# A soft-threshold on ScalarE with its halves moved by transfers, two small routing operations dropped, and more pauses

## The chip, the cores and the metric

The kernel runs on one core of a Trainium2 chip. The metric is the device time of one execution in microseconds; each figure is the median of several. A core has TensorE (PE), VectorE (DVE), ScalarE (ACT), GpSimd (POOL), SyncE (SP) and 16 DMA engines, each engine with its own queue of instructions.

## The reference

Three parts follow each other. The second and third are called moe and moe2 in the code.

```python
X = np.fft.rfft(x, axis=1)                      # x: 8 batches x 3072 x 256
Yr = Xr @ w_r - Xi @ w_i + b_r                  # Yi alike
Yr = np.sign(Yr) * np.maximum(np.abs(Yr) - 0.01, 0.0)
y = np.fft.irfft(Yr + 1j * Yi, n=3072, axis=1)  # 24576 tokens x 256
h = np.maximum(y @ w_in, 0.0)                   # 256 x 2048
z = h * h @ w_out                               # 2048 x 256
logits = z @ w_gate                             # 8 experts
# the first `capacity` (768) tokens of each expert, in order of tokens, keep a slot
out[i] = gate_w[i] * (np.maximum(z[i] @ w1[e], 0.0) @ w2[e])   # kept tokens; else 0
```

## The kernel before

The FFT of a batch runs as two matrix stages with a turn through DRAM between them, the inverse likewise: s1 (x to u), s2 (u to the complex spectrum, `a` and `sm`), mix_a and mix_b (the products with w_r and w_i and the soft threshold, result y), sa (y to z) and sb (z to yT, the tokens of the batch). A batch has 24 indices j for s2 and sa, and 12 pairs k of them for the mix. The first half of the mix (mix_a) adds the bias on VectorE, the second (mix_b) adds its products, so that t = [128, 2, 256] holds the real and the imaginary part. The soft threshold is t - clip(t): VectorE clips t into c (L373), and four GpSimd subtractions of 64x256 (L378) write the halves of t - c, moved to other partitions, into two tiles y. The program's name for the ring of y is `xc`, for t and c it is `ue`, since they share memory with other rings.

The tokens go through in 48 blocks of 512, six a batch. For each block, 16 times (f), l1 makes 128 rows of h: six matmuls, then ScalarE's Relu (L556) and Square (L557). Blocks 0 to 10 are full: l2 follows for each f. From block 11 on a block is late: only the logits are made, by l2_gate, which takes four f at a time (at f=6, 10 and 14, and the last four at f=2 of the next block), twelve bf16 matmuls (L596). They read h*h in three parts: the top half of its bits, what VectorE's first subtraction leaves (L560), and what a second subtraction leaves of that (L561); in the latter, E_POOL names the f that GpSimd does, the others are VectorE's. Both subtractions are emitted one f later (DELAY). route works out the slots of the block before in some 25 small operations, five per f, and four scatters (L663, indirect DMAs issued by GpSimd) follow at f=9.

The FFT of the next batch runs between the l1 of the blocks. A list of steps is handed out by fft_share at an even pace over the blocks of a batch, so that the last step falls at f=6 of the batch's last block; in late blocks f=2, 5 and 10 have no step, and theirs follow at the block's end. From batch 2 on the steps begin at the third block of a batch. So the first two blocks of batches 2 to 5 have no FFT steps; here they are called bare. The list is written by fft_ahead (s1, then load_first, which loads the first spectrum tiles `uj`, then GAP empty steps) and fft_mid (for each pair: two s2, two sa of the pair two before, mix_a, mix_b; some empty steps at the end). Every engine works through its queue in order, so the order of the steps is the order of the work. When all experts are full, the rest is skipped: here the kernel leaves the blocks at f=9 of block 31.

In late blocks l1 has three PSUM tiles, and the FFT steps, route and the transposes share four in turn.

Of the kernel before, what the change touches and what calls it, by code (L numbers as in the profile page):

```python
# [8 lines left out]
F32 = mybir.dt.float32  # L9
F32R = mybir.dt.float32r  # L10
BF16 = mybir.dt.bfloat16
I32 = mybir.dt.int32
U32 = mybir.dt.uint32
AF = mybir.ActivationFunctionType
ALU = mybir.AluOpType
AX = mybir.AxisListType
# [3 lines left out]
P = 128  # L20
N1, N2 = 96, 32
LAM = 0.01
BLK = 512
# [4 lines left out]
def fft_mix__moe__moe2_kernel(  # L28
# [20 lines left out]
    nc = tc.nc  # L49
# [26 lines left out]
    UEX = 1  # L76
    SKIP = ((2, 5, 10), (14, 15))
    E_POOL = (0, 1, 2, 4, 5, 6, 8, 9, 10, 12, 13, 14)
    FROM = 2
    FFT_END = 6  # L80
    GAP = 6
    NPRE = 4
    MV = 4
    OUT_FIRST = (1, 2, 3)
# [38 lines left out]
    one = big.tile([P, P], BF16, name="one")  # L123
    desc = big.tile([P, E], F32, name="desc")
    ebase = big.tile([P, E], F32, name="ebase")
    tid = big.tile([P, TPB], I32, name="tid")
    cnt = big.tile([P, E], F32, name="cnt")
    lcnt = big.tile([P, 1], F32, name="lcnt")
    nlate = big.tile([P, 1], I32, name="nlate")
    oh5 = big.tile([P, TPB + 1, E], BF16, name="oh5")  # L130
    kp5 = big.tile([P, TPB + 1], BF16, name="kp5")
    flag = big.tile([P, 1], I32, name="flag")

    class Fft:
        pass
# [216 lines left out]
    def mix_b(st, k, which):  # L352
        a, sm = st.ab.pop(k)
        p = psum_tile(which)
        t = st.t
        if k == 0:
            products(
                p[0:64, D:2 * D],
                0,
                lambda l, h: a[:, l, 2 * h:2 * h + 2, :].rearrange("p r c -> p (r c)")[:, ::4],  # L360
            )
        products(p[:, 0:D], 0, lambda l, h: sm[:, l, h, :])
        nc.vector.tensor_tensor(
            t, p[:, 0:D].unsqueeze(1).to_broadcast([P, 2, D]), t, op=ALU.add
        )
        if k == 0:
            for r in range(2):
                q = slice(32 * r, 32 * r + 1)
                nc.vector.tensor_tensor(
                    t[0:1, r, :], p[q, D:2 * D], bias[q, 0, :], op=ALU.add  # L370
                )
        c = r_c()
        nc.vector.tensor_scalar(c, t, -LAM, LAM, op0=ALU.max, op1=ALU.min)  # L373
        for n in range(2):
            y = r_y()
            src = slice(64 * n, 64 * n + 64)
            for r in range(2):
                y_eng[n == r].tensor_tensor(  # L378
                    y[64 * r:64 * r + 64, :], t[src, r, :], c[src, r, :], op=ALU.subtract
                )  # L380
            st.y[2 * k + n] = y

# [151 lines left out]

    rest_q = []

    def l1(ys, f, late=False, n_tok=BLK, hook=None):
        yh, yl = ys
        p = psum_tile(1)[:, 0:n_tok]
        order = [(0, yh, 0), (0, yh, 1), (1, yh, 0), (1, yh, 1)]  # L540
        low = [(0, yl, 0), (0, yl, 1)]
        order = low + order if f == KF - 1 else order + low
        for n, (l, y, k) in enumerate(order):
            nc.tensor.matmul(  # L544
                p,
                wi_s[:, l, k, f * P:(f + 1) * P],
                y[:, k, 0:n_tok],
                start=(n == 0),
                stop=(n == 5),
            )  # L550
        if hook:
            hook()
        if late:
            s, d = W.ls(), W.ld()
            e = top(d, 0)
            nc.scalar.activation(s, p, AF.Relu)  # L556
            nc.scalar.activation(s, s, AF.Square)  # L557

            def rests():
                nc.vector.tensor_tensor(d, s, top(s), op=ALU.subtract)  # L560
                (gp if f in E_POOL else ve).tensor_tensor(e, d, top(d), op=ALU.subtract)  # L561

            rest_q.append(rests)
            if len(rest_q) > DELAY:
                rest_q.pop(0)()
            return top(s), top(d), e
        s = W.wk3.tile([P, n_tok], F32, tag="s", name="s")
        nc.scalar.activation(s, p, AF.Relu)  # L568
        sh = W.wk3.tile([P, n_tok], F32R, tag="d", name="sh")
        sl = W.wk3.tile([P, n_tok], F32R, tag="d", name="sl")  # L570
        nc.scalar.activation(sh, s, AF.Square)  # L571
        nc.vector.tensor_tensor(s, s, s, op=ALU.mult)  # L572
        nc.vector.tensor_tensor(sl, s, sh.bitcast(F32), op=ALU.subtract)  # L573
        return sh, sl
# [15 lines left out]
    def top(t, w=1):  # L590
        return t.bitcast(BF16).rearrange("p (n w) -> p n w", w=2)[:, :, w]
# [44 lines left out]
    def small(shape, dt, tag):  # L636
        return W.wk1.tile([P] + shape, dt, tag=tag, name=tag)
# [43 lines left out]
    def route(i, zt, lg, lt):  # L681
# [4 lines left out]
        def op(f, *a, **k):  # L686
            ops.append(lambda: f(*a, **k))  # L687
# [41 lines left out]
        op(v.tensor_reduce, sm, w, axis=AX.X, op=ALU.add)  # L729
        op(v.tensor_scalar, sm, sm, 1e-9, None, op0=ALU.add)  # L730
        op(v.reciprocal, zt[:, :, D], sm)
        op(v.tensor_scalar, zi[:, :, D + 1], tid, i * BLK, None, op0=ALU.add)
        ops += [None, places]
        op(v.scalar_tensor_tensor, ok, pos[:, 0:TPB, :], float(cap), oh, op0=ALU.is_lt, op1=ALU.mult)
        if lt is not None:
            kf = small([TPB], F32, "kf")
            op(v.tensor_reduce, kf, ok, axis=AX.X, op=ALU.add)
            op(v.tensor_copy, kp5[:, 0:TPB], kf)
        op(v.tensor_copy, cnt, pos[:, TPB, :])
        op(v.tensor_reduce, mn, cnt, axis=AX.X, op=ALU.min)  # L740
        op(v.tensor_scalar, flag, mn, float(cap), None, op0=ALU.is_lt)
# [79 lines left out]
    def setup_c():  # L821
        nc.gpsimd.memset(zero, 0.0)
        nc.vector.memset(oh5, 0.0)
        nc.vector.memset(kp5, 0.0)
        nc.vector.memset(lcnt, 0.0)
        nc.vector.memset(nlate, 0)
        nc.vector.memset(cnt, 0.0)
        nc.vector.memset(flag, 1)
        nc.vector.memset(one, 1.0)
        nc.vector.memset(wgate, 0.0)  # L830
        nc.gpsimd.memset(tri, 1.0)
        nc.gpsimd.affine_select(
            out=tri, in_=tri, pattern=[[1, P]], compare_op=ALU.is_gt, fill=0.0,
            base=0, channel_multiplier=-1,
        )
        for e in range(E):
            nc.gpsimd.memset(desc[:, e:e + 1], float(E - e))
            nc.gpsimd.memset(ebase[:, e:e + 1], float(e * cap - BIG))
        nc.gpsimd.iota(tid, pattern=[[P, TPB]], base=0, channel_multiplier=1)

    def late_rows(c, rows):
        nc.sync.dma_start(
# [70 lines left out]
    def fft_mid(st):  # L913
        NP = NJ // 2
        nothing = [lambda: None] * 2

        def a2(j):
            if j % 2 == 0 and 2 <= j < NJ - 2:
                load_j(st, j + 2)
            s2(st, j, 0)  # L920

        def sa2(j):
            sa(st, j, 0)
            if j % 2 and j + 5 < NJ:
                load_m(st, j + 5)

        def both(f, k):
            return [lambda j=2 * k + n: f(j) for n in range(2)]

        seq = both(a2, 0) + nothing  # L930
        for k in range(NP):
            if k + 1 < NP:
                seq += both(a2, k + 1)
            seq += both(sa2, k - 2) if k >= 2 else nothing
            seq += [lambda k=k: mix_a(st, k, 0), lambda k=k: mix_b(st, k, 0)]
        return seq + nothing + both(sa2, NP - 2) + both(sa2, NP - 1)

    def sb_steps(st):
        def step(c):
# [21 lines left out]
    with tc.manual_schedule():  # L961
# [165 lines left out]
        for i in range(NBLK):  # L1127
# [23 lines left out]
            for f in range(KF):  # L1151
                hook = None
                if i + 1 < NBLK:
                    if f == (KF - 3 if o + 1 < BPB else KF - 1):
                        split_y(i + 1, 0)
                    if f == KF - 1:
                        hook = lambda i=i: split_y(i + 1, 1)
                q.append(l1(ys[i], f, not full, hook=hook))
                if i == 0 and f == 0:
                    combine_w()  # L1160
                if f == CARRY and carry:
# [347 lines left out]
```

## Time and profile before

| | |
|---|---|
| median of 3 runs | 2134.39 us (2128.96 to 2148.33) |
| the profiled execution | 2143.82 us, span 2142.1 us |
| mean granted clock of TensorE | 0.978 |
| busy share of the span | PE 96%, DVE 63%, ACT 52%, POOL 39% |

The span goes from the first to the last instruction. Busy is the time in which an engine works on an instruction; waiting for another engine or a transfer isn't counted. The granted clock is the share of full speed (2.4 GHz) that TensorE was given.

### The profile page before, as it was taken

What the parts mean: (1) busy time and instruction counts of PE and PEld (TensorE: products, weight loads), DVE (VectorE), ACT (ScalarE), POOL (GpSimd) and SP (SyncE); (2) the same over time, 40 slices, a digit from 0 to 9 for tenths busy, and PEclk for the clock granted to TensorE, in tenths of its full rate; (3) what the DMA queues carried; (4) which work ended last, traced back from release to release, by engine and by line L of the source; (5) the groups of instructions that cost most, each with busy time, mean ns of one, the idle gap of its engine ahead of it and who ended that gap; (6) DMA issues with size and microseconds to landing.
All of it is one profiled execution on the core that took longest, in us unless ns stands there. A gap on an engine that the chain in (4) does not pass through costs nothing. (4 is left out here: it accounts for less than half of the span.)

```text
span 2142.1 us, 35586 instructions
## 1 busy us (share of the span) xinstructions
PE 2046.2 (96%) x13201; PEld 1746.3 (82%) x13201; DVE 1350.4 (63%) x2621; ACT 1112.5 (52%) x2211; POOL 825.7 (39%) x795
## 2 busy tenths in 40 slices
PE   6899999999999999999999999999999899899998
PEld 3878999998899897667776677766777799899997
DVE  2855666654566665868768588676886666434342
ACT  4644444444544445766557655676556555434331
POOL 2641222120022224637746467464764210244441
PEclk8978999999999999999999999999999999999999
DMA  9758365113211112142221422223221100533200
GB/s 269 230 175 329 124 220 179 48 50 110 86 38 51 41 36 75 30 136 69 66 72 33 131 65 66 71 57 110 76 73 49 58 21 26 166 99 114 97 19 26
DMA packets 155992, 203.10 MB, mean 95 GB/s; under 512 B 13998, under 2 KB 131044, under 8 KB 155794
## 3 DMA queue, kind: packets, MB, share of 16 engines
q1 hardware_dynamic: 139570, 160.07, 24.5%
q0 software_dynamic: 10848, 21.63, 3.2%
q10 hardware_dynamic: 5376, 18.88, 2.6%
q8 instruction: 110, 1.80, 0.3%
q14 instruction: 88, 0.72, 0.1%
HBM read 110.61 MB, written 99.97 MB: 98 GB/s over the span
## 5 line engine op out<-in xcount | busy, mean ns | idle before, releaser
L544 PE MATMUL ph<-yh,wi_s 128*128 128x512 f32 (+1 forms) x1780 | 503.0, 405 | 3.3 <-ACT yh L530 1.6
L561 POOL TENSOR_TENSOR ld<-ld 128x512 bf16<-128x512 f32 x247 | 281.3, 1151 | 336.1 <-DVE ld L560 153.3
L544 PEld LDWEIGHTS ph<-yh,wi_s 128*128 128x128 f32 x1780 | 311.3, 190 | 83.5 <-issue 18.7
L378 POOL TENSOR_TENSOR xc<-ue 64x256 f32<-64x256 f32 x240 | 214.2, 893 | 361.7 <-DVE ue L373 273.1
L560 DVE TENSOR_TENSOR ld<-ls 128x512 f32<-128x512 f32 x329 | 288.4, 882 | 81.9 <-ACT ls L557 69.8
L581 PE MATMUL acc<-wo_s,sh 128*128 128x264 f32 (+1 forms) x1792 | 337.5, 285 | 0.0
L572 DVE TENSOR_TENSOR s<-s 128x512 f32<-128x512 f32 (+1 forms) x272 | 167.9, 617 | 221.4 <-ACT sh L571 221.1
L581 PEld LDWEIGHTS acc<-wo_s,sh 128*128 128x128 f32 x1792 | 286.4, 188 | 12.8
L544 PE MATMUL ph<-yl,wi_s 128*128 128x512 f32 (+1 forms) x890 | 271.6, 386 | 0.0
L581 PE MATMUL acc<-wo_s,sl 128*128 128x264 f32 (+1 forms) x896 | 254.5, 284 | 0.7 <-DVE sl L573 0.7
L568 ACT ACTIVATE s<-ph 128x512 f32<-128x512 f32 (+1 forms) x224 | 123.1, 550 | 234.5 <-PE ph L544 233.6
L557 ACT ACTIVATE ls<-ls 128x512 f32<-128x512 f32 x330 | 208.7, 632 | 10.5
L556 ACT ACTIVATE ls<-ph 128x512 f32<-128x512 f32 x221 | 131.4, 594 | 137.0 <-PE ph L544 131.4
L544 PEld LDWEIGHTS ph<-yl,wi_s 128*128 128x128 f32 x890 | 163.4, 190 | 39.1 <-issue 4.1
L573 DVE TENSOR_TENSOR sl<-s,sh 128x512 fp32r<-128x512 f32 (+1 forms) x272 | 171.9, 632 | 20.0 <-PE ph L544 0.5
L581 PEld LDWEIGHTS acc<-wo_s,sl 128*128 128x128 f32 x896 | 168.7, 188 | 1.5 <-DVE sl L573 1.3
L663 POOL DMA_INDIRECT disp<-zt x54 | 56.0, 1037 | 282.3 <-DVE zt L687 111.9
L544 PE MATMUL acc<-yh,wi_s 128*128 128x512 f32 (+1 forms) x628 | 160.9, 378 | 0.0
L571 ACT ACTIVATE sh<-s 128x512 fp32r<-128x512 f32 (+1 forms) x272 | 151.4, 557 | 8.6
L1401 ACT ACTIVATE rh<-pg 128x384 fp32r<-128x384 f32 x128 | 62.7, 490 | 166.0 <-PE pg L1392 165.2
L1416 PE MATMUL po<-w2s,rh 128*128 128x256 f32 x768 | 139.1, 284 | 0.0
L1392 PE MATMUL pg<-xh,w1s 128*128 128x384 f32 x512 | 136.7, 339 | 0.0
(295 smaller groups left out, 3769.4 us busy)
## 6 DMA issues: line engine op xcount, KB each, us to landing
out_dram<-zero SPq DMA_DIRECT2D x48, 512.0 KB, 5.3
uj<-u SPq DMA_DIRECT2D x72, 256.0 KB, 3.3
z<-ue SPq DMA_DIRECT2D x72, 256.0 KB, 2.2
xc<-z SPq DMA_DIRECT2D x48, 384.0 KB, 3.7
u<-ue ACTq DMA_DIRECT2D x43, 384.0 KB, 4.0
xc<-in_x_dram SPq DMA_DIRECT2D x36, 384.0 KB, 5.1
m<-table SPq DMA_DIRECT2D x72, 128.0 KB, 3.8
ma<-table SPq DMA_DIRECT2D x72, 128.0 KB, 2.5
```

The source lines that it names most:

```text
L378: y_eng[n == r].tensor_tensor(y[64 * r:64 * r + 64, :], t[src, r, :], c[src, r, :], op=ALU.subtract)
L544: nc.tensor.matmul(p, wi_s[:, l, k, f * P:(f + 1) * P], y[:, k, 0:n_tok], start=(n == 0), stop=(n == 5),)
L556: nc.scalar.activation(s, p, AF.Relu)
L557: nc.scalar.activation(s, s, AF.Square)
L560: nc.vector.tensor_tensor(d, s, top(s), op=ALU.subtract)
L561: (gp if f in E_POOL else ve).tensor_tensor(e, d, top(d), op=ALU.subtract)
L571: nc.scalar.activation(sh, s, AF.Square)
L572: nc.vector.tensor_tensor(s, s, s, op=ALU.mult)
L573: nc.vector.tensor_tensor(sl, s, sh.bitcast(F32), op=ALU.subtract)
L581: nc.tensor.matmul(acc[t][:, 0:width], a[:, t * P:(t + 1) * P], wo_s[:, m, f, 0:width], start=(f == 0 and n == 0), stop=(f == KF - 1 and n ...
L1392: nc.tensor.matmul(p[:, 0:gs], w1s[:, l, k, f * P:(f + 1) * P], y[:, k, g * gs:(g + 1) * gs], start=(n == 0), stop=(n == 5),)
L1416: nc.tensor.matmul(acc, a[:, t * P:(t + 1) * P], w2s[:, m, f, :], start=(n == 0), stop=(n == 3 * KD - 1),)
```

## The change

mix_b no longer clips. ScalarE writes relu(t - 0.01) into c and relu(-t - 0.01) into t, GpSimd subtracts them in one pass of 128x512, and move_y copies the four quarters by DMA, issued by SyncE, into the two tiles y. move_y of a pair stands ahead of the first s2 of the next one, so one step after its mix_b. At the end of fft_mid it has a step of its own, and four empty steps stand ahead of the last two sa, where two stood further up. GAP is 8 instead of 6. In blocks in which no FFT step is left, the second subtraction of f=8, 9 and 10 is VectorE's (E_BARE). In route the row of token indices comes from an iota on GpSimd instead of an addition on VectorE, and a sum with a cast behind it became one maximum.

```diff
+    E_BARE = (0, 1, 2, 4, 5, 6, 12, 13, 14)
-    GAP = 6
+    GAP = 8
...
         c = r_c()
-        nc.vector.tensor_scalar(c, t, -LAM, LAM, op0=ALU.max, op1=ALU.min)
+        nc.scalar.activation(c, t, AF.Relu, bias=lam)
+        nc.scalar.activation(t, t, AF.Relu, bias=lam, scale=-1.0)
+        nc.gpsimd.tensor_tensor(c, c, t, op=ALU.subtract)
+        st.c = c
+
+    def move_y(st, k):
         for n in range(2):
             y = r_y()
-            src = slice(64 * n, 64 * n + 64)
             for r in range(2):
-                y_eng[n == r].tensor_tensor(
-                    y[64 * r:64 * r + 64, :], t[src, r, :], c[src, r, :], op=ALU.subtract
+                nc.sync.dma_start(
+                    out=y[64 * r:64 * r + 64, :], in_=st.c[64 * n:64 * n + 64, r, :]
                 )
             st.y[2 * k + n] = y
...
-                (gp if f in E_POOL else ve).tensor_tensor(e, d, top(d), op=ALU.subtract)
+                (gp if f in on_pool else ve).tensor_tensor(e, d, top(d), op=ALU.subtract)
...
-        op(v.tensor_scalar, zi[:, :, D + 1], tid, i * BLK, None, op0=ALU.add)
+        op(
+            nc.gpsimd.iota, zi[:, :, D + 1],
+            pattern=[[P, TPB]], base=i * BLK, channel_multiplier=1,
+        )
...
-            kf = small([TPB], F32, "kf")
-            op(v.tensor_reduce, kf, ok, axis=AX.X, op=ALU.add)
-            op(v.tensor_copy, kp5[:, 0:TPB], kf)
+            op(v.tensor_reduce, kp5[:, 0:TPB], ok, axis=AX.X, op=ALU.max)
...
+        def move_then(k, f):
+            def step():
+                move_y(st, k)
+                f()
+
+            return step
+
         seq = both(a2, 0) + nothing
         for k in range(NP):
-            if k + 1 < NP:
-                seq += both(a2, k + 1)
+            nxt = both(a2, k + 1) if k + 1 < NP else list(nothing)
+            if k:
+                nxt[0] = move_then(k - 1, nxt[0])
+            seq += nxt
             seq += both(sa2, k - 2) if k >= 2 else nothing
             seq += [lambda k=k: mix_a(st, k, 0), lambda k=k: mix_b(st, k, 0)]
-        return seq + nothing + both(sa2, NP - 2) + both(sa2, NP - 1)
+        return (
+            seq + [move_then(NP - 1, lambda: None)] + both(sa2, NP - 2) + nothing
+            + nothing + both(sa2, NP - 1)
+        )
...
-                q.append(l1(ys[i], f, not full, hook=hook))
+                share = E_POOL if steps else E_BARE
+                q.append(l1(ys[i], f, not full, hook=hook, on_pool=share))
```

The line numbers differ between the two kernels: l1 is L544 before and L549 now, the mix L337 and L338, sa L387 and L392, the two subtractions L560 and L561 before and L565 and L566 now, the scatters L663 and L668.

VectorE in the bare block 18, from f=8 on, before. `ld` and `ls` are the parts of h*h, one numbered tile for each f.

```order
L560 TENSOR_TENSOR ld_8104<-ls_8097 128x512
L762 COPY lcnt<-lp 128x1
L763 CAST nlate<-lp 128x1
L1199 TENSOR_LOAD flag
L1118 COMPARE_AND_BRANCH
L560 TENSOR_TENSOR ld_8105<-ls_8098 128x512
L560 TENSOR_TENSOR ld_8106<-ls_8099 128x512
L560 TENSOR_TENSOR ld_8107<-ls_8100 128x512
L561 TENSOR_TENSOR ld_8107<-ld_8107 128x512
L560 TENSOR_TENSOR ld_8108<-ls_8101 128x512
```

The same place now.

```order
L565 TENSOR_TENSOR ld_8179<-ls_8172 128x512
L566 TENSOR_TENSOR ld_8179<-ld_8179 128x512
L769 CAST nlate<-lp 128x1
L1218 TENSOR_LOAD flag
L1136 COMPARE_AND_BRANCH
L565 TENSOR_TENSOR ld_8180<-ls_8173 128x512
L566 TENSOR_TENSOR ld_8180<-ld_8180 128x512
L565 TENSOR_TENSOR ld_8181<-ls_8174 128x512
L566 TENSOR_TENSOR ld_8181<-ld_8181 128x512
L565 TENSOR_TENSOR ld_8182<-ls_8175 128x512
L566 TENSOR_TENSOR ld_8182<-ld_8182 128x512
L565 TENSOR_TENSOR ld_8183<-ls_8176 128x512
```

The second subtraction of f=8, 9 and 10 now follows the first on VectorE; before, only that of f=11 did.

GpSimd in the same block, before: the scatters are the row of L663.

```order
L561 TENSOR_TENSOR ld_8104<-ld_8104 128x512
L663 DMA late<-zt_1540,li_1545 6144x259 x4
L1199 TENSOR_LOAD flag
L1118 COMPARE_AND_BRANCH
L561 TENSOR_TENSOR ld_8105<-ld_8105 128x512
L561 TENSOR_TENSOR ld_8106<-ld_8106 128x512
L561 TENSOR_TENSOR ld_8108<-ld_8108 128x512
```

The same place now.

```order
L566 TENSOR_TENSOR ld_8183<-ld_8183 128x512
L566 TENSOR_TENSOR ld_8184<-ld_8184 128x512
L668 DMA late<-zt_1540,li_1545 6144x259 x4
L1218 TENSOR_LOAD flag
L1136 COMPARE_AND_BRANCH
L566 TENSOR_TENSOR ld_8183<-ld_8183 128x512
```

Before, the parts of f=9 and 10 (8105, 8106) stand behind the scatters; now the first part behind them is that of f=12.

TensorE at the end of the FFT in block 17, from the last mix_b on, before. `s` feeds mix_b, `xc` is y, `ma_109` belongs to the last pair, whose y comes from this mix_b; route's four transposes (L701) stand ahead of these rows.

```order
L337 MATMUL acc_1533<-wmix,s_113 128x256 x6
L544 MATMUL ph<-yh_1538,wi_s 128x512 x4
L544 MATMUL ph<-yl_1539,wi_s 128x512 x2
L387 MATMUL px<-xc_98,ma_108 128x256
L544 MATMUL acc_1531<-yh_1538,wi_s 128x512 x4
L544 MATMUL acc_1531<-yl_1539,wi_s 128x512 x2
L387 MATMUL px<-xc_98,ma_108 128x256
L387 MATMUL acc_1532<-xc_98,ma_109 128x256
```

The same place now; L706 are the four transposes.

```order
L338 MATMUL px<-wmix,s_113 128x256 x6
L549 MATMUL ph<-yh_1538,wi_s 128x512 x4
L549 MATMUL ph<-yl_1539,wi_s 128x512 x2
L706 MATMUL px<-idt,lt_1544 128x128 x4
L392 MATMUL acc_1532<-xc_98,ma_108 128x256
L392 MATMUL acc_1533<-xc_98,ma_108 128x256
L549 MATMUL ph<-yh_1538,wi_s 128x512 x4
L549 MATMUL ph<-yl_1539,wi_s 128x512 x2
L549 MATMUL acc_1531<-yh_1538,wi_s 128x512 x4
L549 MATMUL acc_1531<-yl_1539,wi_s 128x512 x2
L549 MATMUL ph<-yh_1538,wi_s 128x512 x4
L549 MATMUL ph<-yl_1539,wi_s 128x512 x2
```

The last mix_b stands one l1 earlier, and four l1 instead of two lie between it and the first sa that reads its y, which follows these rows.

ScalarE at the end of block 16, before: Relu and Square of an l1, two sa, then the evacuation of s2 (`a`, `ai`, `s`).

```order
L557 ACTIVATE ls_8100<-ls_8100 128x512
L390 ACTIVATE ue_101<-acc_1532 128x256
L390 ACTIVATE ue_101<-acc_1533 128x256
L275 ACTIVATE a_111<-acc_1532 128x512
L276 ACTIVATE ai_114<-acc_1532 128x256
L469 ACTIVATE s_113<-sf_115 128x256
```

The same place now; L374 and L375 are the two new passes.

```order
L562 ACTIVATE ls_8175<-ls_8175 128x512
L374 ACTIVATE ue_100<-ue_100,lam 128x512
L375 ACTIVATE ue_100<-ue_100,lam 128x512
L276 ACTIVATE a_111<-px 128x512
L277 ACTIVATE ai_114<-px 128x256
L474 ACTIVATE s_113<-sf_115 128x256
```

The evacuation of s2 now stands behind the two passes of mix_b.

## Rows read from the trace of the kernel before

**Rows 1.** the page: busy time of each engine
```profile
PE 2046.2 (96%) x13201; PEld 1746.3 (82%) x13201; DVE 1350.4 (63%) x2621; ACT 1112.5 (52%) x2211; POOL 825.7 (39%) x795
```

**Rows 2.** the waits of TensorE: us in total, times, the longest
```profile
PE acc L596 <- POOL ld L561: 14.4, 15, 3.4
...
PE px L337 <- DVE sf L278: 5.4, 3, 1.8
...
PE acc L337 <- DVE sf L278: 5.3, 3, 1.8
...
PE acc L387 <- POOL xc L378: 4.2, 2, 2.4
...
PE acc L262 <- DMA uj<-u: 2.8, 3, 1.4
...
PE px L387 <- POOL xc L378: 2.2, 1, 2.2
...
PE px L262 <- DMA uj<-u: 1.7, 3, 1.3
```

**Rows 3.** timeline of TensorE (start, us, line, idle before): block 11, then block 18
```profile
825.72 0.59 PE L596 MATMUL acc<-ld,wgate 128*32 128x512 bf16 x1 [3.43 <-POOL ld L561]
...
1130.49 0.40 PE L596 MATMUL acc<-ls,wgate 128*32 128x512 bf16 x1
...
1131.29 1.20 PE L544 MATMUL acc<-yh,wi_s 128*128 128x512 f32 x4
...
1136.03 1.10 PE L544 MATMUL acc<-yh,wi_s 128*128 128x512 f32 x4
...
1137.53 0.40 PE L596 MATMUL acc<-ls,wgate 128*32 128x512 bf16 x1
...
1140.31 0.74 PE L544 MATMUL ph<-yl,wi_s 128*128 128x512 f32 x2
```

**Rows 4.** timeline of GpSimd in the same stretch of block 18
```profile
1132.67 1.26 POOL L663 DMA_INDIRECT late<-zt,li  x1 [0.15 <-issue]
...
1137.87 3.04 POOL L561 TENSOR_TENSOR ld<-ld 128x512 bf16<-128x512 f32 x3
```

**Rows 5.** timeline of VectorE in the same stretch of block 18
```profile
1134.29 0.69 DVE L560 TENSOR_TENSOR ld<-ls 128x512 f32<-128x512 f32 x1 [1.22 <-ACT ls L557]
...
1135.01 0.77 DVE L561 TENSOR_TENSOR ld<-ld 128x512 bf16<-128x512 f32 x1
```

**Rows 6.** windows at three ends of an FFT: width, PE busy, granted clock
```profile
1075.00:1080.00 5.00, 3.96 (x15) 0.70 0.15 52
...
1335.00:1340.00 5.00, 3.93 (x15) 0.66 0.15 52
...
1595.00:1600.00 5.00, 4.29 (x19) 0.66 0.15 52
```

**Rows 7.** groups by line and shape: count | busy, mean ns | idle before
```profile
L561 POOL TENSOR_TENSOR ld<-ld 128x512 bf16<-128x512 f32 x247 | 281.3, 1151 | 336.1 <-DVE ld L560 153.3 <-DVE nlate L763 75.5 <-DVE sm L687 61.4
...
L378 POOL TENSOR_TENSOR xc<-ue 64x256 f32<-64x256 f32 x240 | 214.2, 893 | 361.7 <-DVE ue L373 273.1 <-PE ph L544 73.3 <-issue 1.3
...
L560 DVE TENSOR_TENSOR ld<-ls 128x512 f32<-128x512 f32 x329 | 288.4, 882 | 81.9 <-ACT ls L557 69.8 <-PE acc L596 4.2 <-PE px L227 3.4
...
L557 ACT ACTIVATE ls<-ls 128x512 f32<-128x512 f32 x330 | 208.7, 632 | 10.5
```

**Rows 8.** DMA issues of the page (KB, us to landing), and SyncE's timeline
```profile
z<-ue SPq DMA_DIRECT2D x72, 256.0 KB, 2.2
...
997.28 0.47 SPq L242 DMA_DIRECT2D uj<-u  x1
```

**Rows 9.** window of late FFT blocks: busy PE, PEld, DVE, ACT, POOL
```profile
1500.00:1600.00 100.00, 93.96 (x603) 75.92 (x606) 84.16 (x146) 57.31 (x119) 72.83 (x76) 0.98 0.24 71
```

**Rows 10.** timeline at the end of the FFT in block 17
```profile
1072.52 0.68 DVE L363 TENSOR_TENSOR ue<-acc,ue 128x512 f32<-128x512 f32 x1
...
1076.04 0.70 PE L387 MATMUL acc<-xc,ma 128*128 128x256 f32 x2 [1.82 <-POOL xc L378]
```

More of the change, by code (lines that the diff above doesn't have):

```diff
@@ L125, in fft_mix__moe__moe2_kernel @@
     ebase = big.tile([P, E], F32, name="ebase")
-    tid = big.tile([P, TPB], I32, name="tid")
     cnt = big.tile([P, E], F32, name="cnt")
@@ L132, in fft_mix__moe__moe2_kernel @@
     flag = big.tile([P, 1], I32, name="flag")
+    lam = big.tile([P, 1], F32, name="lam")
     class Fft:
@@ L535, in fft_mix__moe__moe2_kernel, with l1 @@
     rest_q = []
-    def l1(ys, f, late=False, n_tok=BLK, hook=None):
+    def l1(ys, f, late=False, n_tok=BLK, hook=None, on_pool=E_POOL):
         yh, yl = ys
@@ L828, in setup_c @@
         nc.vector.memset(flag, 1)
+        nc.vector.memset(lam, -LAM)
         nc.vector.memset(one, 1.0)
@@ L838, in setup_c @@
             nc.gpsimd.memset(ebase[:, e:e + 1], float(e * cap - BIG))
-        nc.gpsimd.iota(tid, pattern=[[P, TPB]], base=0, channel_multiplier=1)
     def late_rows(c, rows):
```

## The prediction, made before the changed kernel ran

> **What bounds the kernel now.** I read the page's busy times first, then the waits of TensorE, then timelines and clock windows around those waits. TensorE is busy for 2046.2 us of a span of 2142.1 us [rows 1]; no other engine is over 63%. So a change that gives TensorE neither less work nor more can move the time only through the 96 us in which it waits, and through what those waits do to its clock. About a third of the 96 us lies ahead of the first block, where the change has no part: the first FFT there keeps its own routine (mix_first). What it can touch lies in the late blocks, between 800 and 1675 us, and the waits of TensorE list it [rows 2]: 14.4 us in 15 waits of the gate matmul (L596) for GpSimd's third part `ld` (L561); 5.4 and 5.3 us in six waits of mix_a (L337), put down to VectorE's `sf` (L278); 4.2 and 2.2 us in three waits of the inverse step (L387) for GpSimd's y (L378); 2.8 and 1.7 us in six waits for `uj`. I asked for these waits in windows of 50 us: the gate's come twice in each of the seven bare blocks that reach f=14 (12, 13, 18, 19, 24, 25, 30), and once, with 3.43 us, in block 11 [rows 3]; the waits for y come once at the end of each late FFT.
>
> **The bare blocks: E_BARE.** In block 18 an undisturbed gate takes 0.80 us from its first matmul to the next group (1130.49 to 1131.29). The gate at f=14 takes 2.78 us (1137.53 to 1140.31) [rows 3]. GpSimd shows why: its scatters of the block before run from 1132.67 on, and the parts of f=9 and f=10 stand behind all four of them; they start at 1137.87, after the gate has begun [rows 4]. The change gives f=8, 9 and 10 to VectorE, where no scatter stands. VectorE then has for each of four l1 in a row one subtraction of 0.69 and one of 0.77 us [rows 5], 1.46 us together, while TensorE takes 1.50 us for an l1 (1136.03 to 1137.53) [rows 3]. Continuing its timeline by these durations, the part of f=11, the last that the gate reads, ends about 1136.2, 1.3 us ahead of the gate. So the cover is thin but there. Gain: 7 x (2.78 - 0.80) = 13.9 us. The wait of 3.43 us in block 11 stays: there it is f=6 that stands behind the scatters, and f=6 is in E_BARE too.
>
> **The end of each FFT: transfers, one more pause.** Before, the inverse step of the last pair waits for four GpSimd passes, 1.82 us at 1076.04 [rows 10], 6.4 us over three FFTs [rows 2]. Behind each of them the granted clock falls: the 5 us windows there show 0.70, 0.66 and 0.66 [rows 6], part of each at 1.2 GHz instead of 2.4, which costs 5 x (0.30 + 0.34 + 0.34) = 4.9 us. Together 11.3 us. After, the chain from the last mix_b is: VectorE's add 0.68 [rows 10]; two ScalarE passes, for which I take the Square from SBUF of the same shape, 2 x 0.63 [rows 7]; one GpSimd pass, between one 128x512 pass (1.15) and today's four (4 x 0.89 = 3.57) [rows 7], and I take 1.2, since the shape is that of the first; two transfers issued at 0.47 each and a landing like that of the z store, 2.2 us for 256 KB [rows 8] (here 64 KB). That is 6.3 us for the first tile, 7.2 us for the second. In the new order (shown above) four transposes, two inverse steps and four l1 stand between mix_b and the first read; 4 x 1.50 alone is 6.0, with the small ones some 7 us. So the chain just fits. I keep 0.8 us of wait for each of the three, too short for the clock in my guess: gain 11.3 - 2.4 = 8.9 us. The bounds are 0 and 11.3.
> Only the page has a price for the bias as an operand: the Trainium skill, ScalarE: Activation LUTs, What ACT_TABLE_LOAD costs, gives a pass with a per-partition bias 280 ns and 0.833 ns per element, 0.71 us here as an estimate. By it the chain would be 6.5 us and the wait 0.2 us longer at each end.
>
> **Two more pauses before the FFT's middle.** GAP = 8 puts load_first further ahead of the first s2. The pauses also make the pace denser: 110 steps instead of 105 in the same blocks, so the first s2 stays where it was among the l1 and the load moves ahead by about two l1, 3 us. The six waits for `uj` are 1.4 us at most: gain 4.5 us, the bounds 2 and 4.5.
>
> **The waits on sf.** Here mix_a reuses the PSUM tile that s2 wrote, and s2's last reader on VectorE is late. Half of them stand at the second pair of each FFT, where the order of l1, prefix and mix_a is the same in both kernels; there VectorE gets earlier (no clip, no cast) and ScalarE later (two passes, 1.26), and I leave them at their 5 us. The other three stand where route meets the mix one block later; the denser pace moves mix_a there one l1 away from s2. I count these 5.3 us as gone.
>
> **What ScalarE and SyncE pay.** ScalarE gets 120 passes, 76 us over five FFTs. Between 200 and 750 us l1 and l2 of the full blocks hide that: none of the waits above lies there. In the late FFT blocks the passes stand in order ahead of the evacuation of s2 and of the Relu of the next l1. Three PSUM tiles for l1 and three l1 between two mixes cover that, except in the burst at a block's end, where six or seven steps follow each other without an l1: there mix_b takes the tile whose evacuation now stands behind two passes (the order on ScalarE above). I charge 1.1 us for each of three such bursts, 3.3 us; the bounds are 0 and 1.8 us (the longest sf wait [rows 2]) for each of twelve late FFT blocks, 22 us. On SyncE four transfers a mix, 1.9 us of issue [rows 8], stand ahead of the loads of `uj` for the next pair, which have an iteration of some 9 us to land. The dropped token-index operation and cast lie on VectorE beside matmuls; I cost them, the iota and the new memset at nothing.
>
> **Sum.** 13.9 + 8.9 + 4.5 + 5.3 - 3.3 = 29.3 us. The profiled execution took 2143.8 us, so 2114.5; the median of the runs shown is 2134.4, 0.4% lower than that execution, which gives 2114.5 x 0.9956 = **2105 us**.
>
> **Rivals.** (a) *ScalarE's queue becomes the bound (slower).* Both passes wait for VectorE's add, and every Relu and Square of l1 stands behind them. If TensorE loses 1.8 us at each of the 36 mixes in late blocks, that is 65 us: 2143.8 - 29.3 + 65, or 2170 at the median's level. From 0.8 us a mix on, all gain is eaten. For it: the in-order queue, and that VectorE is 84% busy from 1500 to 1600 us. Against: ScalarE is 57% busy there [rows 9], and GpSimd's hold on VectorE gets shorter.
> (b) *The transfer takes the place of the wait.* If landing takes 2 us longer than I took, the ends of the FFTs stay as they are: 2105 + 8.9 = 2114.
> (c) *VectorE is late at f=14 in place of GpSimd.* The cover of 1.3 us goes if another VectorE step slips in; no gain in the bare blocks: 2119.
> (d) *More goes.* VectorE's subtraction takes 0.69 us undisturbed [rows 5] and 0.88 in the mean [rows 7], longest where GpSimd works; each mix takes some 2.4 us of GpSimd's work away. If that is what delays `sf`, the other sf waits, the rest of the ends and my ScalarE charge go too: 5.4 + 2.4 + 3.3 more, 2094. The Trainium skill, SBUF — State Buffer, Who interferes with whom, says that a VectorE operation with two SBUF inputs and a GpSimd operation that reads SBUF exclude each other for a whole instruction; the trace agrees with the 0.69 against 0.88 us, and by that rule (d) would be the likelier the more of VectorE's delay is GpSimd's.
>
> **Chances and range.** Forecast (2097 to 2113) 0.55; (a) 0.07; (b) 0.15; (c) 0.08; (d) 0.15. The range goes down to 2090 and up to 2126, which takes in (b), (c), (d) and half of ScalarE's bound; about two in ten lie outside. Runs of this kernel differ by nearly 1% among themselves, so 1% (2113) is about what a measurement can tell from no change. Faster by over 1%: most of the forecast and all of (d), 0.65; within 1%: (b), (c) and the forecast's edge, 0.28; slower by over 1%: (a), 0.07.
>
> **What would show it.** The gate at f=14 in bare blocks takes 0.8 us again, and the gate's waits shrink to the one in block 11. The waits for y stand against a DMA, under 1 us each, and the clock windows there read 1.00. No wait for `uj`. Three sf waits remain. I am wrong if TensorE shows waits for ScalarE in the late FFT blocks, or for VectorE's `ld` at f=14.

## The result, and the profile after

The changed kernel takes 2164.47 us (median of 14 runs, 2148.94 to 2170.56), the kernel before in the same session 2144.43 (14 runs). The ratio is 1.010, with a 95% interval of 1.008 to 1.013: slower by 1%, where 2105 us had been forecast. The profiled execution has a span of 2165.4 us, 23.3 more than before.

The page's busy line of the changed kernel, beside [rows 1]:

```profile
PE 2054.3 (95%) x13201; PEld 1754.3 (81%) x13201; DVE 1268.3 (59%) x2545; ACT 1192.1 (55%) x2331; POOL 653.6 (30%) x611
```

VectorE and GpSimd have less to do, ScalarE more, and the end is later. The 96 us in which TensorE waits became 111, and its busy time grew by 8 us with the same instructions, so part of them ran at a lower clock (the mean granted clock is 0.974, before 0.978). The waits of TensorE say where; they answer to [rows 2].

```profile
PE acc L263 <- DMA uj<-u: 13.8, 6, 4.8
PE px L263 <- DMA uj<-u: 12.2, 5, 3.9
PE px L338 <- DVE sf L279: 6.7, 4, 2.3
PE px L706 <- ACT lt L638: 4.8, 4, 1.8
PE acc L338 <- DVE sf L279: 3.9, 3, 2.3
PE acc L601 <- POOL ld L566: 2.3, 1, 2.3
PE px L263 <- ACT ue L374: 1.9, 1, 1.9
PE acc L706 <- ACT lt L638: 1.8, 1, 1.8
...
PE acc L392 <- DMA xc<-ue: 0.4, 2, 0.2
PE px L392 <- DMA xc<-ue: 0.3, 1, 0.3
```

The gate waits once instead of 15 times, and the inverse step at the ends of the FFTs 0.7 us in all instead of 6.4, both as forecast. But s2 waits 26 us for `uj`, where 4.5 had stood and none was expected. The timeline of TensorE in block 18 of the changed kernel confirms the gate: 0.80 us from its first matmul to the next l1, against 2.78 in [rows 3].

```profile
1146.00 0.40 PE L601 MATMUL acc<-ls,wgate 128*32 128x512 bf16 x1
...
1146.80 0.74 PE L549 MATMUL ph<-yl,wi_s 128*128 128x512 f32 x2
```

In windows at the three ends of an FFT the clock is at its full level, where [rows 6] had 0.70, 0.66 and 0.66:

```profile
1083.00:1088.00 5.00, 4.50 (x24) 3.34 (x24) 3.25 (x7) 4.21 (x10) 2.75 (x2) 1.00 0.18 44
...
1352.00:1357.00 5.00, 4.59 (x24) 3.29 (x23) 4.09 (x11) 4.17 (x11) 2.90 (x3) 1.00 0.32 89
1621.00:1626.00 5.00, 4.76 (x24) 3.38 (x23) 4.20 (x11) 4.21 (x10) 2.90 (x3) 1.00 0.33 96
```

So the loss lies elsewhere. A good ruler is the start of each gate in TensorE's timeline, since the gates stand at the same f in every kernel. Outside the late FFTs the intervals between gates, from block 11 to block 31, sum to 393.3 us before and 376.6 after: 16.7 gained. From f=2 of the first to f=6 of the last block of the three late FFTs they sum to 481.5 and 518.8: 37.3 lost. The loss is not spread over the 36 mixes. It sits at a few places, the same in each FFT, most of all at the ends of the FFT's second and third block, where the burst of steps without l1 runs: from the gate at f=14 of the second block to the next gate it is 22.0, 22.9 and 21.8 us in the three FFTs, before 14.0, 13.9 and 14.1. This is the one at the end of block 15, in the changed kernel; first the timeline of ScalarE:

```profile
1007.50 0.72 ACT L374 ACTIVATE ue<-ue,lam 128x512 f32<-128x512 f32 x1 [1.98 <-POOL ld L566]
1008.25 0.72 ACT L375 ACTIVATE ue<-ue,lam 128x512 f32<-128x512 f32 x1
...
1014.34 0.72 ACT L374 ACTIVATE ue<-ue,lam 128x512 f32<-128x512 f32 x1 [1.42 <-DMA xc<-ue]
```

GpSimd's pass on the same tile:

```profile
1009.05 1.30 POOL L376 TENSOR_TENSOR ue<-ue 128x512 f32<-128x512 f32 x1 [1.85 <-ACT ue L375]
```

SyncE's queue, the four transfers and behind them the loads of the next pair's table `m` and of `uj`:

```profile
1010.38 2.38 SPq L383 DMA_DIRECT2D xc<-ue  x4
1012.80 0.59 SPq L242 DMA_DIRECT2D m<-table  x1
1013.43 0.50 SPq L243 DMA_DIRECT2D uj<-u  x1
```

TensorE:

```profile
1011.02 0.87 PE L338 MATMUL acc<-wmix,s 128*128 128x256 f32 x6
1016.66 1.19 PE L263 MATMUL acc<-m,uj 128*128 128x128 f32 x4 [4.76 <-DMA uj<-u]
1017.50 2.05 PE L549 MATMUL ph<-yh,wi_s 128*128 128x512 f32 x4
```

Read them as one chain. The passes of one mix end at 1008.97, GpSimd's at 1010.35, and only then can SyncE issue the transfers, 0.59 us each. The load of `uj` stands in the program ahead of the s2 that TensorE ran at 1006.35; it is issued at 1013.43, 7 us later, and the next pair's s2 starts at 1016.66 after 4.76 us of waiting. The windows show the clock behind it: 0.50 from 1015 to 1020, so TensorE worked there at 1.2 GHz of 2.4, and the four l1 matmuls took 2.05 us where four take 1.20 [rows 3].

```profile
1010.00:1015.00 5.00, 1.90 (x12) 1.41 (x10) 4.30 (x8) 2.74 (x6) 0.35 (x1) 0.95 0.36 88
1015.00:1020.00 5.00, 3.34 (x10) 2.89 (x11) 0.00 (x0) 0.79 (x2) 2.26 (x2) 0.50 0.52 152
```

### The profile page after: what moved, and what is told of

The parts are those of the page before. It is cut to its first block, busy times and chain, and to the rows that moved or that the text cites. A ratio compares the mean times of both kernels' runs of the same rounds, so it can differ in the third digit from the quotient of the medians.

```text
span 2165.4 us, 35935 instructions
## 1 busy us (share of the span) xinstructions
PE 2054.3 (95%) x13201; PEld 1754.3 (81%) x13201; DVE 1268.3 (59%) x2545; ACT 1192.1 (55%) x2331; POOL 653.6 (30%) x611
## 5 line engine op out<-in xcount | busy, mean ns | idle before, releaser
L549 PE MATMUL ph<-yh,wi_s 128*128 128x512 f32 (+1 forms) x1780 | 503.5, 406 | 3.7 <-ACT s L573 1.7
L549 PEld LDWEIGHTS ph<-yh,wi_s 128*128 128x128 f32 x1780 | 313.3, 192 | 81.9 <-issue 18.8
L566 POOL TENSOR_TENSOR ld<-ld 128x512 bf16<-128x512 f32 x213 | 238.5, 1124 | 364.6 <-DVE ld L565 202.1
L577 DVE TENSOR_TENSOR s<-s 128x512 f32<-128x512 f32 (+1 forms) x272 | 163.3, 601 | 250.3 <-ACT sh L576 249.8
L565 DVE TENSOR_TENSOR ld<-ls 128x512 f32<-128x512 f32 x329 | 253.1, 773 | 97.0 <-ACT ls L562 80.0
L549 PE MATMUL ph<-yl,wi_s 128*128 128x512 f32 (+1 forms) x890 | 272.9, 388 | 0.9 <-DVE yl L538 0.9
L376 POOL TENSOR_TENSOR ue<-ue 128x512 f32<-128x512 f32 x60 | 77.2, 1286 | 487.2 <-ACT ue L375 485.0
L549 PEld LDWEIGHTS ph<-yl,wi_s 128*128 128x128 f32 x890 | 164.1, 191 | 42.2 <-DVE yl L538 3.2
L561 ACT ACTIVATE ls<-ph 128x512 f32<-128x512 f32 x221 | 131.1, 593 | 108.6 <-PE ph L549 101.7
L578 DVE TENSOR_TENSOR sl<-s,sh 128x512 fp32r<-128x512 f32 (+1 forms) x272 | 162.7, 598 | 20.5 <-DVE s L577 0.5
L549 PE MATMUL acc<-yh,wi_s 128*128 128x512 f32 (+1 forms) x628 | 160.5, 378 | 0.0
L668 POOL DMA_INDIRECT disp<-zt x54 | 58.4, 1082 | 287.4 <-ACT zt L620 104.0
```

The costliest lines, as they stand in the source:

```text
L549: nc.tensor.matmul(p, wi_s[:, l, k, f * P:(f + 1) * P], y[:, k, 0:n_tok], start=(n == 0), stop=(n == 5),)
L566: (gp if f in on_pool else ve).tensor_tensor(e, d, top(d), op=ALU.subtract)
```

## The experiments

Two theories came out of this. **S:** the transfers, which wait for GpSimd, hold SyncE's queue and the loads of `uj` behind them. **A:** the two passes, which wait for VectorE's add and for the transfers out of c, hold ScalarE's queue and with it evacuations (copies out of PSUM) that TensorE needs. The rivals are named with each run. Ratios are to the kernel before in the same session, whose median was 2142.7 to 2145.5 us.

**Loads ahead of the transfers** (e1_load_first).

```diff
-                move_y(st, k)
                 f()
+                move_y(st, k)
```

> The step that moves y first issues the loads of the next uj and only then the four transfers; nothing else differs from the changed kernel. Theory S (on SyncE the transfers, which wait for GpSimd's pass, stand ahead of the loads of uj): the waits of TensorE for uj fall from 26 us to under 5 us, the clock dips behind them go, time about 2135 us (30 less than the changed kernel). Theory A (the passes on ScalarE hold up what stands behind them): at most 5 us less, the waits move to another name. Theory P (the denser pace and the burst at a block's end): no change.

Measured: 2153.07 us, 1.002 (0.9997 to 1.0046). The waits for `uj` are gone, and 11 of the 20 us lost are back. But other waits grew: for `lt` from 6.6 to 15.1 us, for `sf` from 10.6 to 17.4. The waits of TensorE in this run:

```profile
PE px L338 <- DVE sf L279: 10.6, 8, 2.4
PE px L706 <- ACT lt L638: 10.3, 4, 3.9
PE acc L338 <- DVE sf L279: 6.8, 7, 2.3
PE acc L706 <- ACT lt L638: 4.8, 2, 3.0
```

ScalarE's timeline in this run at the end of block 15 shows the new holder:

```profile
1008.34 0.63 ACT L562 ACTIVATE ls<-ls 128x512 f32<-128x512 f32 x1
1011.46 0.72 ACT L374 ACTIVATE ue<-ue,lam 128x512 f32<-128x512 f32 x1 [2.49 <-DMA xc<-ue]
1012.22 0.72 ACT L375 ACTIVATE ue<-ue,lam 128x512 f32<-128x512 f32 x1
1012.85 0.58 ACT L561 ACTIVATE ls<-ph 128x512 f32<-128x512 f32 x1
...
1017.68 0.58 ACT L638 ACTIVATE lt<-acc 128x512 f32<-128x512 f32 x1
```

Two waits make up the 2.49 us in which ScalarE stands still. VectorE's add of this mix, which the passes read, ends at 1010.29:

```profile
1009.61 0.68 DVE L364 TENSOR_TENSOR ue<-acc,ue 128x512 f32<-128x512 f32 x1
```

From then on, until 1011.46, it is c, which is one buffer that the transfers of the mix before still read. Then come 1.4 us of passes, and only then the Relu of an l1, the evacuation of s2 and `lt`, for which TensorE waits:

```profile
1018.31 0.76 PE L706 MATMUL px<-idt,lt 128*128 128x128 f32 x4 [3.88 <-ACT lt L638]
```

**Passes without transfers** (e2_passes_only).

```diff
-        nc.gpsimd.tensor_tensor(c, c, t, op=ALU.subtract)
...
-                nc.sync.dma_start(
-                    out=y[64 * r:64 * r + 64, :], in_=st.c[64 * n:64 * n + 64, r, :]
+                nc.gpsimd.tensor_tensor(
+                    y[64 * r:64 * r + 64, :], c[src, r, :], t[src, r, :], op=ALU.subtract
```

> The two passes on ScalarE stay, but four GpSimd subtractions of 64x256 write y as before; there are no transfers, and move_y is empty. S: no waits for uj, time near that of the run with the loads first, about 2140 us, with some waits for GpSimd at the ends of the FFTs again. A: the waits for lt and for s2 and the clock dips stay, 2155 us or more.

Measured: 2160.87 us, 1.007 (1.003 to 1.010). No waits for `uj`, but 16.1 us for `lt`. Without any transfer the time is nearly that of the whole change.

**Transfers without passes** (e3_clip_and_moves).

```diff
-        nc.scalar.activation(c, t, AF.Relu, bias=lam)
-        nc.scalar.activation(t, t, AF.Relu, bias=lam, scale=-1.0)
-        nc.gpsimd.tensor_tensor(c, c, t, op=ALU.subtract)
+        nc.vector.tensor_scalar(c, t, -LAM, LAM, op0=ALU.max, op1=ALU.min)
+        nc.gpsimd.tensor_tensor(c, t, c, op=ALU.subtract)
```

> VectorE clips as before, one GpSimd pass subtracts, and the transfers stay; ScalarE has no passes. S: the waits for uj stay above 15 us, since GpSimd's pass comes only some 1 us earlier; time 2150 to 2160 us. A: most of the loss goes, about 2135 us, and the waits for lt are gone.

Measured: 2147.61 us, 1.001 (0.9985 to 1.004). Now `lt` is nearly quiet and s2 waits for `uj` alone, as long as in the changed kernel:

```profile
PE px L263 <- DMA uj<-u: 16.2, 7, 3.3
...
PE acc L263 <- DMA uj<-u: 10.5, 3, 3.9
...
PE px L705 <- ACT lt L637: 0.9, 1, 0.9
```

**E_BARE alone**, added to the kernel before (e4_bare_alone).

```diff
-                q.append(l1(ys[i], f, not full, hook=hook))
+                share = E_POOL if steps else E_BARE
+                q.append(l1(ys[i], f, not full, hook=hook, on_pool=share))
```

> The kernel before with E_BARE alone. As predicted, the gate at f=14 of seven bare blocks takes 0.8 instead of 2.8 us: about 14 us less than before, 2130 us. Rival: VectorE is late in place of GpSimd, no change.

Measured: 2131.12 us, 0.993 (0.990 to 0.996), 13.6 us less than before; the gate keeps one wait, 3.4 us, in block 11. That term of the sum is right on its own.

**Neither cause: clip on VectorE, one GpSimd pass, loads first** (e5_clip_load_first; the edits of the first and the third together).

> VectorE clips again, GpSimd still makes one pass, the transfers stay but stand behind the loads of uj. Two causes, each enough alone (S: the transfers hold up SyncE; A: the passes hold up ScalarE): with both gone, the waits of s2 for uj and of the transposes for lt are under 3 us each, and the time is 2110 to 2122 (0.984 to 0.990 of the kernel before). Rival, one cause in two places (the lateness of GpSimd's one pass, which the transfers and the next mix wait for): it is still there, so 2140 to 2155.

Measured: 2110.72 us, 0.985 (0.978 to 0.992). From the changed kernel, removing the transfers' place gained 11 us, removing the passes 17, removing both 54: two causes that cover each other, each enough to spend all that the rest gains (with either one left, the ratios 1.002 and 1.001 can't be told from 1). The fifth has four runs, from 2102.00 to 2120.68, and the profiled one is the slowest of them. Where s2 waits for `uj`, ScalarE gets time to catch up; that is argued, from the waits for `lt`, 6.6 us in the changed kernel and 15.1 in the first experiment.

**The old soft threshold in the changed kernel** (e6_old_shrink): VectorE clips, four subtractions on GpSimd, no transfers.

```diff
+        nc.vector.tensor_scalar(c, t, -LAM, LAM, op0=ALU.max, op1=ALU.min)
...
-                nc.sync.dma_start(
-                    out=y[64 * r:64 * r + 64, :], in_=st.c[64 * n:64 * n + 64, r, :]
+                y_eng[n == r].tensor_tensor(
+                    y[64 * r:64 * r + 64, :], t[src, r, :], c[src, r, :], op=ALU.subtract
```

> The changed kernel with the whole soft threshold of before: clip on VectorE, four GpSimd subtractions, no transfers; E_BARE, the pauses and the two routing edits stay. S and A: nothing of what slows is left, so 2115 to 2128: the 14 us of E_BARE, the waits for uj (about 4) gone, the waits for y at the ends of the FFTs under 2 us since more steps lie ahead of them. Rival, the denser pace of the steps (110 in place of 105) is what makes s2 and the transposes late: then they wait here too, 10 us or more for uj or lt, and the time is over 2130.

Measured: 2122.19 us, 0.991 (0.988 to 0.994). So the pace and the pauses are not to blame. Against this run, which differs from the second in the clip and its two passes alone, the passes cost 38.7 us with no transfer in the kernel. The six kernels side by side, medians in us:

| | two passes on ScalarE | clip on VectorE |
|---|---|---|
| transfers ahead of the loads | 2164.47 (changed) | 2147.61 (third) |
| loads ahead of the transfers | 2153.07 (first) | 2110.72 (fifth) |
| four subtractions, no transfers | 2160.87 (second) | 2122.19 (sixth) |

**Passes two steps later** (e7_passes_later): the passes, GpSimd's pass (now `shrink`) behind the second s2 that follows, the transfers one step on.

```diff
-                nxt[0] = move_then(k - 1, nxt[0])
+                nxt[1] = then(nxt[1], shrink)
...
+                inv[0] = then(inv[0], move_y, k - 1)
```

> ScalarE's two passes and GpSimd's pass are emitted behind the second s2 that follows mix_b, two steps later, and the transfers one step after that, so behind the loads. A (the passes hold what stands behind them because they wait for VectorE's add and for the transfers' read of c): in this place the add is long done, the waits for lt and sf fall from some 33 us of the first experiment to under 15, and the time is 2115 to 2135. Rival (it is the amount of ScalarE's work, 1.45 us a mix, that makes it late): the waits stay, 2145 to 2160. A third outcome, the later GpSimd pass makes the next mix_a's add wait for t: waits of mix_a or mix_b for VectorE, 2140 to 2170.

Measured: 2149.53 us, 1.003 (0.9998 to 1.0065). None of the three outcomes came alone. The waits for `sf` disappeared, those for `lt` fell only to 13.1 us, and the inverse step now waits 20.3 us for the late transfers of y. It doesn't tell A from its rival.

**Four passes** (e8_four_passes; loads first, and two more that repeat the rectifying).

```diff
         nc.scalar.activation(t, t, AF.Relu, bias=lam, scale=-1.0)
+        nc.scalar.activation(c, c, AF.Relu)
+        nc.scalar.activation(t, t, AF.Relu)
```

> As the first experiment (loads first), with two more passes on ScalarE that change nothing (relu of what is already rectified): four passes of 0.72 us a mix. A with a queue that has no slack left: each of 36 late mixes adds up to 1.45 us of lateness, the waits for lt, sf and for VectorE's add behind them grow by 20 us or more, 2175 to 2210. Rival (ScalarE has slack, and the loss in the first experiment is due to the pauses or the transfers): under 2160.

Measured: 2200.16 us, 1.029 (1.022 to 1.036), 47 us over the first experiment for 36 x 2 x 0.72 = 52 us more of ScalarE in the late FFTs. Behind a pass that starts late, each further microsecond is nearly all lost; the two more passes also hold back GpSimd's pass and the transfers, and that share wasn't tried apart.

**The work without the wait** (e9_passes_no_wait) **and the wait without the work** (e10_wait_no_passes), both added to the fifth.

```diff
+        for _ in range(2):
+            nc.scalar.activation(scr, bias.rearrange("p r d -> p (r d)"), AF.Relu, bias=lam)
```

```diff
+        nc.scalar.activation(scr[:, 0:2], c[:, 0, 0:2], AF.Relu, bias=lam)
```

> The fifth experiment (VectorE clips, loads first), with two passes of ScalarE added where the two rectified copies stood; they read the constant bias and write a scratch tile that nobody reads, so they wait for nothing. A as head-of-line (what costs is that a pass waits for VectorE's add with the evacuations queued behind it): 2108 to 2122, as the fifth, since 1.4 us a mix fits into ScalarE's idle third. Rival (the amount: ScalarE's queue has no slack where a mix stands): 2140 to 2160, with waits for lt and sf of 25 us or more, as in the first experiment.

> The fifth experiment with one tiny operation of ScalarE (128x2) added in the passes' place, which reads what VectorE has clipped: ScalarE waits as long as with the passes (a little longer, by the clip's 0.4 us), but pays only some 0.2 us of work. A as head-of-line: most of the 42 us that lie between the first and the fifth experiment come back, 2135 to 2155. Rival (the amount): 2110 to 2122.

Measured: 2117.23 us, 0.9875 (0.985 to 0.990), and 2126.13 us, 0.990 (0.987 to 0.994). With the same 120 passes ScalarE is as busy as in the changed kernel, 1192.8 us, and the time can't be told from that of the fifth, or of the eleventh run beside it (2113.45 us): the amount alone is not the cause. The wait alone costs 13 us against the eleventh, or 15 against the fifth, with two runs at 2118 and two at 2134 us; A as I had put it for these two, as waiting only, had 2135 at least, so it fell as well. ScalarE's timeline of the ninth, again in the burst of block 15, shows why the work costs nothing that can be told when it waits for nothing:

```profile
1002.80 0.63 ACT L564 ACTIVATE ls<-ls 128x512 f32<-128x512 f32 x1
1003.34 1.46 ACT L377 ACTIVATE scr<-bias,lam 128x512 bf16<-128x512 f32 x2
1004.73 0.60 ACT L563 ACTIVATE ls<-ph 128x512 f32<-128x512 f32 x1
...
1009.58 0.58 ACT L640 ACTIVATE lt<-acc 128x512 f32<-128x512 f32 x1
```

The two passes (L377 x2) start right behind the Square, and `lt` starts 6.2 us after that Square's end (1003.43). In the first experiment it starts 8.7 us after it (1008.97 to 1017.68), and the 2.49 us of standing still are nearly all of the difference.

**Block 11 as well** (e11_best): the fifth, and there the part of f=6 is VectorE's.

```diff
-                share = E_POOL if steps else E_BARE
+                share = E_BARE if not steps else E_POOL[:5] + E_POOL[6:] if i == NFULL else E_POOL
```

> The fifth experiment, and in block 11 the part of f=6 is VectorE's as well, so that it doesn't stand behind the scatters: the last wait of the gate for GpSimd, 2.3 us, goes. Both theories: 2106 to 2120, 0.983 to 0.989 of the kernel before; a difference of 2 us to the fifth can't be told, only the wait's absence can.

Measured over five rounds: 2113.45 us, 0.9855 (0.983 to 0.988); the gate has no wait for GpSimd left. This and the fifth beat both kernels.

**Transfers issued by GpSimd** (e12_moves_by_gpsimd; the third, `nc.gpsimd.dma_start` for `nc.sync.dma_start`).

> The third experiment (VectorE clips, one pass on GpSimd, transfers in their place ahead of the loads) with the four transfers issued by GpSimd in place of SyncE. S as a matter of SyncE's queue (the loads stand behind transfers that wait for GpSimd): no waits for uj over 3 us in all, 2108 to 2125. Rival (the transfers' traffic or the late y itself delays the loads or s2): the 26 us of waits for uj stay, 2140 to 2155. A third outcome: the issue of a transfer holds GpSimd long enough that the gates or the ends of the FFTs wait for it.

Measured: 2122.29 us, 0.990 (0.987 to 0.993). The order of the steps is that of the third experiment, yet no wait for `uj` is left in the late FFTs. So it is SyncE's queue, not the transfers' traffic. GpSimd is 126 us busier, y is later, and the inverse step waits 11.9 us for it.

**Wait and work together** (e13_passes_on_t: the ninth with `t` for `bias`; e14_passes_on_c: with `c`, so that GpSimd's pass waits for them too).

> The ninth experiment with passes that read t in place of a constant: ScalarE waits for VectorE's add and then works 1.4 us; nobody waits for the result, so GpSimd's pass, y and the next t are as early as in the fifth. A as wait plus work (the passes start late, and their work then stands ahead of evacuations that are due): most of the 42 us between the first and the fifth come back, 2140 to 2158. Rival (what slows is that GpSimd's pass, and with it t and y, come 1.4 us later): 2115 to 2128, as with the wait alone.

> The same with passes that read the clipped c, which GpSimd overwrites, so GpSimd's pass waits for them as in the changed kernel. A as wait plus work: 2140 to 2162, at most 6 us over the one on t (the clip's 0.4 us more of waiting). Rival (GpSimd's lateness): 2140 to 2160 here and under 2128 on t.

Measured: 2144.72 us, 1.000 (0.997 to 1.003), and 2166.50 us, 1.013 (1.006 to 1.019). In the thirteenth only ScalarE's queue is touched (neither VectorE nor GpSimd shows a wait for the passes), and against the ninth, with the same passes, reading a tile that is ready later costs 27 us. The fourteenth costs 22 more; in it the passes start later, behind the clip and the transfers' read of c, and GpSimd's pass stands behind them. Which of the two weighs more wasn't tried apart.

The sums of the gates' intervals show the places, over the three late FFTs, in us of the profiled executions. Steps shift between the stretches with the pace, so the kernel before compares by the sum alone.

| stretch | before | changed | e1 | e3 | e5 | e9 | e13 |
|---|---|---|---|---|---|---|---|
| first two blocks | 241.1 | 253.6 | 248.4 | 252.0 | 243.6 | 239.2 | 247.7 |
| end of the second | 42.0 | 66.7 | 47.7 | 61.8 | 44.3 | 44.1 | 47.1 |
| third block | 110.3 | 111.3 | 124.2 | 109.2 | 110.9 | 110.8 | 118.5 |
| end of the third | 41.8 | 55.4 | 62.2 | 53.0 | 45.9 | 48.3 | 55.5 |
| fourth, to f=6 | 46.3 | 31.7 | 30.0 | 29.1 | 29.1 | 29.3 | 29.2 |
| sum | 481.5 | 518.8 | 512.6 | 505.1 | 473.7 | 471.7 | 497.9 |

S strikes in the burst itself (e3 against e5, 17.5 us at the end of the second block). A strikes in the burst of the third block and in the l1 that follow the first burst (e1 against e5, 16.3 and 13.3), where late Relus and `lt` meet TensorE.

## Why the prediction was wrong

**Bare blocks, -13.9: right.** 13.6 us by the experiment alone, and the gate at f=14 as forecast. Block 11's wait, counted as staying, shrank to 2.3 us.

**Ends of the FFTs, -8.9: right in size, but not by the transfers.** Waits of 0.7 us where 2.4 were kept, and the clock stayed up. But the second and the sixth experiment, with four GpSimd subtractions and no transfer, show no wait for y there either; the sixth has the clock at 1.00 in these windows too. So the later place of the last inverse steps is enough; that the transfers are needed isn't shown. The parts as the groups of the changed kernel have them (count, busy, mean ns), to set beside [rows 7]:

```profile
L376 POOL TENSOR_TENSOR ue<-ue 128x512 f32<-128x512 f32 x60 | 77.2, 1286 | 487.2 <-ACT ue L375 485.0 <-DVE mx L692 2.2
...
L374 ACT ACTIVATE ue<-ue,lam 128x512 f32<-128x512 f32 x60 | 43.4, 724 | 123.7 <-DVE ue L364 83.1 <-DVE ue L370 14.7 <-DMA xc<-ue 14.4
```

A pass takes 0.72 us (0.63 was taken), GpSimd's 1.29 (1.2), and the page has 2.0 us for the landing (2.2). The Trainium skill's estimate for a pass with a per-partition bias (ScalarE: Activation LUTs, What ACT_TABLE_LOAD costs), 0.71 us, agrees with these 0.72 us; the row that I took had 0.63.

**First loads, -4.5: right in itself.** In the first late FFT the first load is issued 7.0 us ahead of the first s2 (943.15 and 950.17), before 2.8 (950.88 and 953.69), and none of the waits for `uj` in the changed kernel stands at an FFT's first s2. They stand at later pairs, where S puts them. (The lists have 103 and 110 steps; the 105 was miscounted.)

**sf, -5.3: wrong.** The waits were 10.7 us before and are 10.6 after, in the same stretches. The three in the second block of each FFT, to be left as they were, grew from 1.8 to 2.3 us each; the three in the third block, counted as gone, shrank only from 1.8 to 1.0; one of 0.6 is new.

**SyncE, without a term in the sum: the first step that failed.** An issue costs 0.59 us, a little more than the 0.47 taken; what I left out is that a transfer waits in SyncE's queue for GpSimd's pass, and the load of `uj` with it. The "iteration of some 9 us" isn't there in a burst: from 1005.23 to 1011.02 two mix_b follow each other in 5.8 us, while passes, GpSimd, issue and landing take 6.8 (1007.50 to 1014.34; the last transfer lands at 1014.24 and frees c for the next, at a time when VectorE's add of that mix, done at 1014.22, is only just there). With the passes gone, this costs 37 us (third against fifth); with them, 11 (changed against first).

**ScalarE, +3.3: the second.** The place was named, the burst, and the order of the evacuation behind the passes; the size was 42 us (first against fifth; 39 without transfers, second against sixth), over the bound of 22. My own sign of being wrong came true: TensorE waits 6.6 us for `lt`, a result of ScalarE, in the changed kernel. I charged one held evacuation a burst. But a late start is not made up there: it passes through the following Relus to `lt` and `sf`. And the dependence on the transfers through the single buffer c was missing. Rival (a) named this queue and gave nearly the right time, 2170, by a loss at each of 36 mixes; that was luck in part, since the loss is at a few places in each FFT and S is not in it.

**(d): no.** VectorE's first subtraction did get shorter, from 882 ns in the mean [rows 7] to 773:

```profile
L565 DVE TENSOR_TENSOR ld<-ls 128x512 f32<-128x512 f32 x329 | 253.1, 773 | 97.0 <-ACT ls L562 80.0 <-PE acc L601 14.0 <-POOL ld L566 0.5
```

In the kernel before, the 159 that overlap one of GpSimd's two-input operations (TENSOR_TENSOR) take 1.09 us in the mean, the other 170 0.69 us and never over 0.75; after, 85 overlap. That agrees with the rule that (d) named (the Trainium skill, SBUF — State Buffer, Who interferes with whom). But the shorter subtraction didn't reach the end: the sf waits stayed.

Sum: 16.7 us gained outside the late FFTs, 37.3 lost in them, 20.6 of the 23.3 us of span; the rest lies outside this stretch. The base was low as well: three runs of the kernel before had a median of 2134.39 us, fourteen have 2144.43, so 10 of the 59 us between forecast and result come from the base. With both failed steps taken out, the fifth and the eleventh are 32.0 and 30.1 us under the kernel before, near the 29.3 of the sum, though the sum had sf wrong.

## What to carry to other kernels

An instruction put into an in-order queue is priced by when its inputs come, not by its duration: 120 passes cost nothing that these runs can tell while their input was a constant, and some 27 us once they read a tile that was late, with urgent work behind them. Put loads whose inputs are long ready ahead of transfers that wait for another engine, and look for single buffers that such a transfer still reads. Check the cover at the densest stretch of the schedule, not at its mean pace.

## What the hardware showed that was not expected

The issue of a transfer holds SyncE for 0.59 us (four in 2.38), sometimes longer: four took 3.15 us at 1017.18. Issued by GpSimd instead, the 240 transfers raised its busy time from 662.7 to 788.5 us, about 0.52 us each, and TensorE's wait for `uj` vanished.
